# A state-space and gated-MLP block whose first part takes its order and its engines from a table in place of a planner

## The chip, the cores and the metric

One core of a Trainium2 chip. The time is that of one execution on the device in microseconds (us); the lower the better.

## The reference

The input x is 2048 rows of 640 numbers, all in float32. Six rows of modulation (shift, scale and gate, twice) come from one condition vector through a 640 x 3840 matrix. The block is then

```python
h = layernorm(x) * (1 + ca) + sa
x = x + ga * A(h)        # A: a long convolution along the rows, per channel
h = layernorm(x) * (1 + cb) + sb
x = x + gb * B(h)        # B: (silu(h @ w1) * (h @ w3)) @ w2, 640 -> 1728 -> 640
```

A builds, for each of the 640 channels, a kernel of 2048 taps, `K = 2 Re sum_n C[n] exp(A[n] dt l)` over 128 complex terms, convolves the channel with it by Fourier transforms of length 4096, and adds `h * D_skip`.

## The kernel before

The kernel has two parts. The **first part** computes the parameters, layernorm statistics and modulation, and then A for five blocks of 128 channels (b = 0 to 4). The **second part** adds the inverse transform to x, normalises again and does B; its instructions stand in an order of their own.

A block of the first part runs through these steps; the names in brackets are the tiles in the profile.

- *Generation*, eight chunks of 16 channels (`gen_tasks`, `gen_chunk`): GpSimd adds the phases (ph) and multiplies the decay factors out of two small tables (e, into yy and xx); ScalarE takes sines and one absolute value (tr, ph); VectorE does five multiplies (yy, xx); TensorE multiplies 32 pairs into kps; ScalarE copies kps to ks, and VectorE adds the skip term. The chunk's products need all five multiplies. Every tile of the ring (ph, xx, yy, tr, kps) has 2 or 3 buffers.
- *Tables* for the chunks: three sums and three smaller steps per half block (step, p), on GpSimd but for a few that either GpSimd or VectorE does; `al8`, a scaling by the row index (tiles al8, xs_al8, ks0) that ScalarE's exp needs, and `mag`, a product in place, each on GpSimd or VectorE.
- *Normalised input*, four pieces (`h_tasks`): load xq, normalise to hn (four instructions, on ScalarE or VectorE), multiply and add a row on VectorE (hn, hb), store to hs, and fetch all of it turned around into xb.
- *First transform* of h and of K, eight pieces each (`first_tasks`): TensorE to ps, copied to sp by ScalarE or VectorE.
- *Spectra*, eight groups (`spectra_tasks`): TensorE makes fh and fk, ScalarE copies fh to hz, VectorE multiplies them into fp (x0, x1, c), TensorE makes fz out of two groups, and two copies to zt by ScalarE or VectorE, each stored to zd in DRAM.

At the end of the first part, once the last chunk's product is done, `change` frees the generator's memory and issues the loads of the residual rows and of the inverse table (in all five loads, the residual's in four). For the first two weight tiles, 0 and 13, there are tasks for the loads (`fw`, raw tiles wr and w2r), the rounding on ScalarE (`fa`, to wh and w2h) and the subtraction on GpSimd (`fs`, to wl and w2l). `iz` reads zd back for the first rows, four loads each, and `ir` does their inverse on TensorE and adds them on VectorE. Weights 1 and 2 belong to the second part, but their loads stand among the first part's last stores on SyncE.

All first-part work is given as 1532 *tasks* (`Plan.add`): a name, one engine or several to choose from, how long it is taken to last on each, what must come before, a rank, and the buffers it takes and gives. `Plan.place` works out an order: it keeps a clock per engine, one for the port that GpSimd and VectorE share, and one for the DMA line, and of the tasks that could start soonest on each engine it takes the one with the least rank; where a task has two engines it takes the one that would be done first. The durations are constants in the calls of `add`, the ranks a list of 1532 numbers (`RANKS`). `Plan.run` then calls the tasks in that order. Because each engine's instructions are chained as they are called (`InOrder`, whose line 157 all of them bear in the profile), the order of the calls is the order on each engine: an instruction that waits holds up all that stand behind it on its engine.

Of the kernel before, what the change touches and what calls it, by code (L numbers as in the profile page):

```python
# [32 lines left out]
RANKS = """  # L33
# [67 lines left out]
FP = 2  # L101
# [64 lines left out]
class Engines:  # L166
    def __init__(self, k, nc):
        self.vector, self.scalar, self.gpsimd, self.tensor, self.sync = (
            InOrder(k, e) for e in (nc.vector, nc.scalar, nc.gpsimd, nc.tensor, nc.sync))


class Plan:

    LAG = dict(PE=0.2, DVE=0.18, ACT=0.2, POOL=0.15, SP=0.0)
    CHAIN = dict(DVE=0.12, ACT=0.12, POOL=0.07)
    NEAR, RATE, LAND, FLY, ISSUE, AWAY, TABLE = 0.1, 235e3, 1.3, 0.7, 0.06, 8, 1.28

    def __init__(self, **rings):  # L180
        self.tasks, self.n = {}, rings
# [1692 lines left out]
```

## Time and profile before

| | us |
|---|---|
| median of 3 runs | 973.91 (970.91 to 974.12) |
| the profiled execution | 976.3 |
| its span, first to last instruction | 974.5 |
| TensorE busy | 869.6 |
| VectorE busy | 717.6 |
| ScalarE busy | 517.2 |
| GpSimd busy | 334.6 |

In the profile PE is TensorE, PEld its weight loads, DVE VectorE, ACT ScalarE, POOL GpSimd, and SP SyncE, which issues the DMAs; SPq marks SyncE's own queue. A row of a timeline has the start in us, the length in us, the engine, the line, the operation, what it writes and reads, the shapes, and in brackets how long the engine had been idle and what ended that. A row of a group has the number of instructions, their busy time, the mean in ns of one, and the idle time before them. A row of a stretch of time has its limits and length, then the busy time of PE, PEld, DVE, ACT and POOL with the number of instructions, TensorE's granted clock, the DMA engines' busy share and GB/s. The first part takes the first 380 us or so; the generator's last product ends at 345.1 us.

### The profile page before, as it was taken

The page shows a single profiled execution, that of the slowest core. Times are in us where ns is not written, and L with a number is a line of the kernel's source. Part 1 is how long each engine was busy: PE and PEld are TensorE (multiplying, and loading weights), DVE is VectorE, ACT ScalarE, POOL GpSimd, SP SyncE. Part 2 cuts the span into 40 slices and gives each one's busy share as a digit, 9 for nine tenths or more (in the row PEclk, how much of TensorE's full clock was granted, in tenths as well). Part 3 has the DMA queues.
Part 4 walks back from the last instruction along what each step waited for, and adds up shares of the span by engine and source line. Part 5 has one row for each costly group of instructions (what it writes and reads, how often), then busy time and mean ns, then how long its engine had stood idle before and what let it go on. Part 6 is the DMA issues. An engine that isn't in the chain of part 4 may idle for free.

```text
span 974.5 us, 20145 instructions
## 1 busy us (share of the span) xinstructions
PE 869.6 (89%) x8017; PEld 691.6 (71%) x8017; DVE 717.6 (74%) x1300; ACT 517.2 (53%) x866; POOL 334.6 (34%) x345
## 2 busy tenths in 40 slices
PE   1454787879899998999999999999999999999997
PEld 1132665767788883667778888888888888888875
DVE  7998999999999954747775375567477777765763
ACT  6868788979888841522243243445234444445331
POOL 1797798879899512100000000000212222200000
PEclk9886898999999999999999999999999999999999
DMA  9955453722223278987522354223131112122242
GB/s 217 279 167 197 105 136 88 175 65 80 57 67 88 68 207 236 218 214 181 144 82 81 95 148 121 83 81 90 46 82 54 54 54 55 41 81 87 88 151 82
DMA packets 122822, 113.19 MB, mean 116 GB/s; under 512 B 11752, under 2 KB 106472, under 8 KB 121320
## 3 DMA queue, kind: packets, MB, share of 16 engines
q1 hardware_dynamic: 121992, 110.99, 42.2%
q8 instruction: 63, 1.03, 0.4%
q10 hardware_dynamic: 736, 0.92, 0.3%
q14 instruction: 31, 0.25, 0.1%
HBM read 90.91 MB, written 20.97 MB: 115 GB/s over the span
## 4 chain that ended last, share of the span: by engine, by line
PE 68%; DMA 12%; DVE 12%; ACT 4%; issue 3%; SPq 1%; POOL 0%; ACTq 0%; DVEq 0%; POOLq 0%
PE p L875 16%; PE acc L1122 16%; PE gu L1085 6%; PE gu L1087 6%; PE gu L1086 6%; PE ps L157 5%; PE kps L157 3%; DVE yy L157 3%; PE fk L157 3%; PE fz L157 3%; PE fh L157 2%; DMA sp<-in_w_mod 2%; DMA zd<-zt 2%; DMA xs<-in_x 2%; DVE xx L157 2%
## 5 line engine op out<-in xcount | busy, mean ns | idle before, releaser
L1085 PE MATMUL gu<-xh,wh 128*128 128x512 f32 x270 | 105.2, 393 | 0.9 <-ACT xh L667 0.7
L1087 PE MATMUL gu<-xh,wl 128*128 128x512 f32 x270 | 105.3, 390 | 0.0
L1086 PE MATMUL gu<-xl,wh 128*128 128x512 f32 x270 | 105.2, 390 | 0.0
L875 PE MATMUL p<-x,wch 128*128 128x512 f32 x312 | 92.6, 390 | 0.0
L157 POOL TENSOR_TENSOR yy<-e,e 128x512 f32<-128x512 f32 x80 | 86.2, 1095 | 17.5 <-PE kps L157 12.6
L894 POOL TENSOR_TENSOR ws<-wp 128x256 f32<-128x256 f32 x13 | 9.6, 740 | 228.7 <-DVE wcl L668 116.1
L157 POOL TENSOR_TENSOR ph<-p,p 128x1024 int32<-128x1024 int32 x40 | 79.0, 1974 | 5.7 <-ACT tr L157 5.0
L157 PE MATMUL kps<-yy,xx 128*32 128x64 f32 x2560 | 52.1, 238 | 27.3 <-DVE xx L157 24.0
L157 DVE TENSOR_TENSOR yy<-yy,tr 128x512 f32<-128x512 f32 (+1 forms) x80 | 75.3, 943 | 0.9 <-ACT tr L157 0.6
L157 PEld LDWEIGHTS kps<-yy,xx 128*32 128x32 f32 x2560 | 45.6, 118 | 37.0 <-issue 20.6
L779 ACT ACTIVATE wh<-wr 128x640 fp32r<-128x640 f32 x51 | 34.9, 731 | 64.3 <-PE gu L1086 51.6
L875 PEld LDWEIGHTS p<-x,wch 128*128 128x128 f32 x312 | 58.2, 188 | 12.6 <-ACT s L910 0.4
L1085 PEld LDWEIGHTS gu<-xh,wh 128*128 128x128 f32 x270 | 50.6, 188 | 11.7 <-ACT xh L667 1.0
L1087 PEld LDWEIGHTS gu<-xh,wl 128*128 128x128 f32 x270 | 50.7, 188 | 11.1 <-DVE wl L788 0.4
L1086 PEld LDWEIGHTS gu<-xl,wh 128*128 128x128 f32 x270 | 50.7, 188 | 10.5 <-DVE xl L668 0.2
L791 POOL MEMSET w2l<- 64x640 f32 x1 | 0.6, 633 | 165.5 <-PE acc L1122 165.5
L875 PE MATMUL p<-x,wcl 128*128 128x512 f32 x156 | 57.0, 389 | 0.0
L157 ACT ACTIVATE tr<-ph,hpi 128x512 f32<-128x512 f32 x80 | 54.7, 691 | 4.2 <-DVE xx L157 2.5
L157 DVE TENSOR_TENSOR xx<-tr,xx 128x512 f32<-128x512 f32 x80 | 54.3, 680 | 0.8 <-ACT tr L157 0.8
L912 DVE TENSOR_TENSOR s<-p,s 128x512 f32<-128x512 f32 x52 | 34.7, 682 | 26.9 <-ACT s L910 22.9
L157 ACT ACTIVATE tr<-ph 128x512 f32<-128x512 int32 x80 | 47.4, 599 | 12.7 <-DVE yy L157 5.8
L157 PE MATMUL ps<-wk,ks 128*64 128x128 f32 x640 | 41.9, 283 | 13.6 <-DVE ks L157 9.7
(367 smaller groups left out, 2303.1 us busy)
## 6 DMA issues: line engine op xcount, KB each, us to landing
wr<-in_w SPq DMA_DIRECT2D x52, 320.0 KB, 3.7
zd<-zt SPq DMA_DIRECT2D x39, 256.0 KB, 2.8
w2r<-in_w SPq DMA_DIRECT2D x26, 320.0 KB, 3.1
wp<-in_w SPq DMA_DIRECT2D x26, 320.0 KB, 3.2
wq<-in_w SPq DMA_DIRECT2D x26, 320.0 KB, 3.2
low<-zd SPq DMA_DIRECT2D x24, 320.0 KB, 6.6
xs<-in_x SPq DMA_DIRECT2D x16, 320.0 KB, 11.1
hs<-hb SPq DMA_DIRECT2D x20, 256.0 KB, 2.5
```

The costliest lines, as they stand in the source:

```text
L157: self.prev = self.k.order(f(*a, **kw), self.prev)
L779: self.nc.scalar.activation(wh[:, i], raw[:, i], AF.Copy)
L791: self.nc.gpsimd.memset(w2l[64:].bitcast(F32), 0.0)
L875: nc.tensor.matmul(to, t[:, o], y[:, k], start=start and k == i == 0, stop=stop and (k, i) == (n - 1, 2), skip_group_check=True)
L894: G.tensor_tensor(s[0], a21, a22, op=ALU.add)
L912: add = lambda o, bk, s: V.tensor_tensor(o, bk, s, op=ALU.add)
L1085: nc.tensor.matmul(pg, wh[:, k, :], xh[:, k, :], start=(k == 0), stop=False)
L1086: nc.tensor.matmul(pg, wh[:, k, :], xl[:, k, :], start=False, stop=False)
L1087: nc.tensor.matmul(pg, wl[:, k, :], xh[:, k, :], start=False, stop=(k == KT - 1))
L1122: nc.tensor.matmul(acc[k], *two(a, w), start=(m == 0 and i == 0), stop=(m == 12 and i == 2))
```

## The change

The tasks, their buffers and what each waits for stay as they are. The planner, with its durations and ranks, is gone. In place of `RANKS` stands `ORDER`, a list of the 1532 task numbers in the order in which they are called; a letter behind a number tells the engine where a task has a choice (a, d, p: ScalarE, VectorE, GpSimd). Of the table only the first line is shown; its numbers tell a reader nothing.

```diff
-RANKS = """
--1152 -1540 -1534 -1515 -1509 -1417 -1345 -1436 -1412 -1402 -1385 -1330 -1273 -1351 -1452 -1478 -1480 -1475 -1459 -1510 -1507
...
+ORDER = """
+1 2 7 13 79 78 80 4 86 81 41 14 19 82 20 42 84 21 15 83 22 16 150p 85 43 23 151 120 12 44 24 17 10 25 18 3 45 61 28 26 59 30
...
-    def __init__(self, **rings):
-        self.tasks, self.n = {}, rings
+    def __init__(self):
+        self.tasks = {}
...
-    def place(self, rank):
...
     def run(self):
 
-        T = self.tasks
-        found = [int(x) for x in RANKS.split()]
-        assert not found or len(found) == len(T)
-        self.order = self.place(dict(zip(T, found)) if found else {n: t[4] for n, t in T.items()})
-        for s, f, e, n in self.order:
-            if T[n][2]:
-                T[n][2](e)
+        T = list(self.tasks.items())
+        done = set()
+        for x in ORDER.split():
+            n, (engs, f, after) = T[int(x.rstrip("adp"))]
+            assert done.issuperset(after), (n, set(after) - done)
+            done.add(n)
+            if f:
+                f(dict(a="ACT", d="DVE", p="POOL")[x[-1]] if len(engs) > 1 else engs[0])
+        assert len(done) == len(T)
...
-        self.plan = plan = Plan(ph=2, xx=2, yy=2, tr=3, kg=2, f2=3, bank=4, hz=3, xq=2, fp=FP, zt=3, xs=4, st=1)
+        self.plan = plan = Plan()
```

What the table does to the queues: 54 tasks change engine. VectorE gets 13 more of the copies from ps to sp (it had 19 and gives back five for 18), six of the zt copies while four go to ScalarE, and loses nine normalisations for two. The scalings al80 and al81 go to GpSimd and al82 and al84 come to VectorE, with mag4; of the table copies three go to GpSimd and two come. On VectorE, the last piece of h for block 4 stands 64 us of its work earlier, by the traced durations. Nothing moves in the second part's own order. Three places follow in full.

The first is ScalarE at the end of the first part, in the kernel before. hz40 to hz47 are the copies of block 4's eight groups, zt401 the copy of its first fz; wh0_0 and wh0_13 are the roundings of weight tiles 0 and 13.

```order
L157 ACTIVATE hz40_4914<-fh40_4889 128x512
L157 ACTIVATE hz41_4937<-fh41_4916 128x512
L157 ACTIVATE hz42_4961<-fh42_4941 128x512
L157 ACTIVATE hz43_4974<-fh43_4951 128x512
L157 ACTIVATE zt400_5000<-fz400_4976 128x512
L157 ACTIVATE hz44_5024<-fh44_5004 128x512
L157 ACTIVATE hz45_5047<-fh45_5028 128x512
L157 ACTIVATE wh0_0_5049<-wr0_0_4864 128x640 x2
L157 ACTIVATE w2h0_0_5050<-w2r0_0_4867 128x640
L157 ACTIVATE hz46_5094<-fh46_5069 128x512
L157 ACTIVATE wh0_13_5102<-wr0_13_4899 128x640
L157 ACTIVATE w2h0_13_5103<-w2r0_13_4902 128x640
```

And the same place in the kernel after:

```order
L146 ACTIVATE hz40_4914<-fh40_4895 128x512
L146 ACTIVATE hz41_4925<-fh41_4905 128x512
L146 ACTIVATE wh0_13_4936<-wr0_13_4854 128x640
L146 ACTIVATE w2h0_13_4937<-w2r0_13_4857 128x640
L146 ACTIVATE hz42_4969<-fh42_4943 128x512
L146 ACTIVATE hz43_4981<-fh43_4958 128x512
L146 ACTIVATE wh0_0_4985<-wr0_0_4879 128x640 x2
L146 ACTIVATE w2h0_0_4986<-w2r0_0_4882 128x640
L146 ACTIVATE zt401_5026<-fz401_5003 128x512
L146 ACTIVATE zt400_5030<-fz400_5002 128x512
L146 ACTIVATE hz44_5033<-fh44_5017 128x512
L146 ACTIVATE zt410_5065<-fz410_5045 128x512
```

Weight 13 is now rounded behind the second hz copy and weight 0 behind the fourth; before, weight 0 stood behind the sixth and weight 13 behind the seventh.

The second place is SyncE from the loads that `change` issues on, in the kernel before. low<-in_x and low<-in_t_wd are the residual rows and the inverse table, wr and w2r the raw weights (of tiles 0, 13, 1 and 2), low<-zd the loads of iz, four each, and zd<-zt the stores of block 4.

```order
L157 DMA low_4848<-in_x 32x2560 x4
L157 DMA low_4848<-in_t_wd 128x2048
L157 DMA wr0_0_4864<-in_w1 128x5x128
L157 DMA wr0_0_4864<-in_w3 128x5x128
L157 DMA w2r0_0_4867<-in_w2 128x640
L157 DMA wr0_13_4899<-in_w1 128x5x64
L157 DMA wr0_13_4899<-in_w3 128x5x64
L157 DMA w2r0_13_4902<-in_w2 64x640 x2
L157 DMA low_4848<-zd_71 64x2x512 x4
L157 DMA zd_71<-zt400_5000 128x4x128
L157 DMA zd_71<-zt401_5002 128x4x128
L157 DMA zd_71<-zt410_5066 128x4x128
```

Behind these stand iz's other four loads, weight 1's three and then zt411's store. In the kernel after, from weight 0's w2 on:

```order
L146 DMA w2r0_0_4882<-in_w2 128x640
L665 DMA wr0_1_5429<-in_w1 128x5x128
L665 DMA wr0_1_5429<-in_w3 128x5x128
L670 DMA w2r0_1_5432<-in_w2 128x640
L146 DMA zd_71<-zt401_5026 128x4x128
L146 DMA zd_71<-zt400_5030 128x4x128
L665 DMA wr0_2_5519<-in_w1 128x5x128
L665 DMA wr0_2_5519<-in_w3 128x5x128
L670 DMA w2r0_2_5522<-in_w2 128x640
L146 DMA zd_71<-zt410_5065 128x4x128
L146 DMA low_4848<-zd_71 64x2x512 x8
L146 DMA zd_71<-zt411_5094 128x4x128
```

Weight 13's loads now stand ahead of weight 0's, both still directly behind the five loads of `change`; weight 1's loads stand ahead of block 4's first store and weight 2's ahead of the third; and all eight loads of iz stand in one piece between the third store and the fourth (zt411, the task z4.1.o1). On TensorE and VectorE the two units of `ir` move from the middle of block 4's last groups to behind its last fz.

The third place is VectorE in the first block, chunks 5 and 6 (tiles with 80 and 96 in their names; tr4 marks a chunk's last multiply). Before:

```order
L157 SCALAR_TENSOR_TENSOR yy_96_809<-yy_96_809,tr0_96_823 128x16x32
L157 TENSOR_TENSOR hn_814<-hn_814,rw_87 128x512
L157 TENSOR_TENSOR yy_96_809<-yy_96_809,tr0_96_823 128x16x32
L157 TENSOR_TENSOR xx_96_808<-tr1_96_826,xx_96_808 128x512
L157 TENSOR_TENSOR hb01_844<-hn_728,rw_87 128x512
L157 TENSOR_TENSOR yy_96_809<-yy_96_809,tr3_96_842 128x1024
L157 TENSOR_TENSOR xs_al8_851<-al_126,j8_103 128x1024
L157 TENSOR_TENSOR hb02_858<-hn_814,rw_87 128x512
L157 TENSOR_TENSOR xx_80_734<-tr4_80_833,xx_80_734 128x512
```

And after:

```order
L146 TENSOR_TENSOR hn_658<-hn_658,rw_87 128x512
L146 TENSOR_TENSOR yy_80_708<-yy_80_708,tr3_80_810 128x1024
L146 TENSOR_TENSOR hb01_820<-hn_658,rw_87 128x512
L146 TENSOR_TENSOR xx_80_707<-tr4_80_813,xx_80_707 128x512
L146 TENSOR_TENSOR xx_96_804<-tr1_96_822,xx_96_804 128x512
L146 SCALAR_TENSOR_TENSOR yy_96_805<-yy_96_805,tr0_96_817 128x16x32
L146 TENSOR_TENSOR ks0_128<-kps_410,dsk_74 128x4 x2
```

Chunk 5's last multiply stood behind four multiplies of chunk 6 and the scaling of block 1 (xs_al8); now it stands ahead of all of chunk 6, and that scaling is on GpSimd.

More of the change, by code (lines that the diff above doesn't have):

```diff
@@ new lines @@
+851 589 329a 461 467 464 590 339a 469 591 354 449 584 465 326 475 454 355a 470 466 455 327a 471 492 479 334 593d 456 480 472
+335a 481 476 457 585 866 356 594 473 477 482 373 484 357 586 595 478 358 474 485 596 852a 493 486 375 359 494 487 483 856 496
+495 488 374 501 497 509 489 597 867a 360 503 361 510 490 502 861 362 498 491 376 511 853 363 512 499 377 513 854 701 500 504
+855 364 519 514 505 515 702 378 506 520 526 862a 365 518 366 527 516 868 530 367 529 517 535 507 528 508 522 521 543 536 523
@@ new lines @@
+406 411 575 735 404 736 576 725 721 733 1138 737 559 412 1139 415 734 722 741 1141a 608 416 727 614 609a 417 1414 615a 743 738
+418 1399 742 616 1142 739 1143 723 744 740 1144 602 749 617a 728 1415a 612 745 766 603d 729 613d 753 1130 626 1416 1400a 752
+1417 746 627d 1418 975 770 624 1401 1125 754 1402 419 755 760 1403 1131d 625a 978p 769 618 422a 423 976 420d 619a 1409 1132
+979 1126a 606 977 1133 607d 421 598 1134 750 1127 628 599a 751 1128 758 1129 604 1410a 767 629d 759 600 980 775 605a 768 981
@@ new lines @@
+662a 661 828 687 823 663 673 681 674 688 824 675 814 985p 682 983 829 825 683 835 815 830 838 676 684 989 839 843 840 816 685
+689 841 677d 837 679a 686 678 831 836 680 690 896 845 832 986 1247 691 987 892 897d 984 692 890 893d 990 693 988 891d 833 844
+992 846 876 991 993 694d 894 1248d 695 886 696d 877a 999 994 697 884 895d 842 1000 995 1006 874 847 887a 998 848 1145 875a
+885d 996 898 849 1007 1001 997 904 1010 1009 1002 1011 900 850 1015 905 1008 899d 1012 902 1023 901d 1003 1013 1016 903a 1017
@@ new lines @@
+1244a 1362 1242a 1223 1245 1373 1243 1377 1438 1363 1385 1386 1378 1436 1445a 1383 1439d 1387 1379 1437a 1393 1384 1388 1391
+1224 1392 1380 1389 1381 1364 1390 1394 1446 1227a 1395 1440 1228 1447a 1225d 1396 1441d 1226 1448 1397 1398 1520 1525 1450
+1449d 1426 1522 1451a 1442 1521 1427d 1452 1443d 1458 1453 1454 1459 1460 1526 1455 1456 1469 1461 1527 1475 1457 1470 1462
+1471 1476 1463 1523 1472 1477 1473 1464 1474 1524 1478 1479 1486 1467a 1480 1465a 1468 1487 1466 1488 1481 1489 1490 1491 1492
@@ L99 @@
+1482a 1483 1503 1493 1528 1494 1504 1484a 1495 1530 1505 1496 1509 1497 1506 1511 1510 1485 1507 1512 1508 1513 1498 1514 1515
+1501a 1499d 1500 1502 1529 1518a 1519 1516a 1531 1517
 """
@@ L172 @@
 class Plan:
-    LAG = dict(PE=0.2, DVE=0.18, ACT=0.2, POOL=0.15, SP=0.0)
-    CHAIN = dict(DVE=0.12, ACT=0.12, POOL=0.07)
-    NEAR, RATE, LAND, FLY, ISSUE, AWAY, TABLE = 0.1, 235e3, 1.3, 0.7, 0.06, 8, 1.28
-    def __init__(self, **rings):
-        self.tasks, self.n = {}, rings
+    def __init__(self):
+        self.tasks = {}
     def add(self, name, eng, took, f, after=(), rank=0.0, port=False, take=(), give=(), table=None, dma=None):
         assert name not in self.tasks, name
-        take = [(r, name + "".join(x), k) for r, k, *x in take]
@@ L272, in run @@
-    def run(self):
-        T = self.tasks
-        found = [int(x) for x in RANKS.split()]
-        assert not found or len(found) == len(T)
-        self.order = self.place(dict(zip(T, found)) if found else {n: t[4] for n, t in T.items()})
-        for s, f, e, n in self.order:
-            if T[n][2]:
-                T[n][2](e)
+            eng, f = (eng,), f and (lambda e, f=f: f())
+        self.tasks[name] = (eng, f, tuple(after))
+    def run(self):
+        T = list(self.tasks.items())
[7 more added lines that the diff above has]
+        assert len(done) == len(T)
```

115 lines of the change are left out of this document (35 added, 80 removed), and 64 rows, old and new, of the table RANKS.

## The prediction

> **What bounds the kernel now.** I read the page first, then the busy times by stretch, then the chain of waits from 340 us on, and last the single instructions of VectorE, ScalarE and the DMA queue around the places where the new order differs.
>
> ```profile
> span 974.5 us, 20145 instructions
> PE 869.6 (89%) x8017; PEld 691.6 (71%) x8017; DVE 717.6 (74%) x1300; ACT 517.2 (53%) x866; POOL 334.6 (34%) x345
> ```
>
> The execution took 976.3 us, 1.8 more than its span and 2.4 (0.25%) more than the median, 973.91. I add differences to the median. The three runs before lie 3.2 us apart, so about 0.5% (4.9 us) is the least that a measurement tells from no change.
>
> The averages hide two halves. These are the busy times of the first part, in four stretches:
>
> ```profile
> 0.00:20.00 20.00, 1.30 (x5) 0.93 (x5) 13.83 (x35) 11.89 (x23) 1.68 (x19) 1.00 0.92 199
> 20.00:120.00 100.00, 55.66 (x920) 36.30 (x922) 92.18 (x175) 77.15 (x146) 81.60 (x77) 0.81 0.66 194
> 120.00:280.00 160.00, 134.60 (x2754) 113.00 (x2754) 152.87 (x286) 136.44 (x230) 141.11 (x142) 0.96 0.39 99
> 280.00:340.00 60.00, 59.42 (x1218) 49.10 (x1208) 58.57 (x106) 50.59 (x89) 49.91 (x46) 1.00 0.29 73
> ```
>
> The third figure after the stretch's length is VectorE (the order is PE, weight load, VectorE, ScalarE, GpSimd). From 20 to 340 us VectorE is idle for 7.8 + 7.1 + 1.4 = 16.4 us in all. It is the bound, and TensorE joins it from 280 us on (59.4 of 60). So a new order can win at most 16.4 us of waits there, plus what VectorE no longer has to do before the last generated chunk is ready. After that a second regime begins, in the chain of waits:
>
> ```profile
> 344.03 1.10 PE kps L157 x61
> 362.88 0.70 DVE zt L157
> 364.09 5.65 DMA zd<-zt
> 369.81 7.25 DMA zd<-zt
> 377.13 0.60 ACT zt L157
> 378.07 6.04 DMA zd<-zt
> 384.85 3.48 DMA low<-zd
> 388.46 1.51 PE iy L653 x10
> ```
>
> The last product of the generator ends at 345.1 (kps, 344.03 + 1.10). Block 4 then runs through its spectra (fh, fk, fz), and the chain passes to the stores of zd: a copy out of fz waits until an older store has released its zt buffer. The last store lands at 384.1, 39.0 us after that product, and only then can the feed-forward part read zd. What follows is issued in the same order in both kernels, so I take it as unchanged. The forecast is the sum of two shifts: that of the last product, and that of the 39.0 us.
>
> **The work VectorE does ahead of the last product.** Durations by kind, 0 to 400 us:
>
> ```profile
> L157 DVE COPY sp<-ps 128x512 f32<-128x512 f32 x19 | 12.7, 682 | 2.6 <-PE ps L157 2.5
> L157 DVE TENSOR_SCALAR hn<-xq,rs_y_h,rs_n_h 128x128 f32<-128x128 f32 x44 | 18.1, 412 | 1.6 <-ACT sp L157 0.3
> L157 DVE TENSOR_TENSOR xs_al<-al,j 128x1024 f32<-128x1024 f32 x1 | 2.8, 2817 | 0.0
> L157 DVE TENSOR_TENSOR ks<-al,j 128x1024 f32<-128x1024 f32 x1 | 1.2, 1218 | 0.0
> L157 DVE TENSOR_TENSOR e<-e,mag 128x512 f32<-128x512 f32 x2 | 2.2, 1077 | 0.0
> L157 DVE TENSOR_SCALAR p<-pB 128x128 int32<-128x128 int32 x4 | 1.1, 273 | 0.0
> ```
>
> The new table gives VectorE 13 more copies out of ps and 4 more out of fz ahead of block 4's spectra, and leaves 5 of these 17 behind its last generator multiply: 12 x 0.68 = +8.2 us. It takes away 7 normalisations of four instructions: 7 x 4 x 0.412 = -11.5. Two scalings by the row index (al8) leave, 1.22 and 2.82, and two come back for later blocks; I price these at the mean, 2.02 each, so they cancel (between 1.22 and 2.82 each, that is -1.6 to +1.6). One magnitude product comes, +1.1, and one of the copies of p goes, -0.3. Sum -2.5; ScalarE takes the other side and has room (136 of 160 us). Instructions overlap by some 0.06 us, so **-2.4**.
>
> The 2.82 us stand beside running GpSimd work, the 1.22 us where GpSimd was idle. The Trainium skill, SBUF — State Buffer, section on the two separate sides, says that VectorE and GpSimd share one port pair under an exclusive lock, which an instruction of VectorE with two SBUF inputs also needs; these rows agree. By that rule both scalings would come back at 2.82 and the term would be -0.8.
>
> **The start.** The rows of GpSimd and ScalarE where the first chunk begins:
>
> ```profile
> 34.14 2.28 POOL L157 TENSOR_TENSOR ph<-p,p 128x1024 int32<-128x1024 int32 x1
> 36.45 0.60 ACT L157 ACTIVATE tr<-ph 128x512 f32<-128x512 int32 x1 [0.56 <-POOL ph L157]
> ```
>
> and two groups of the first 400 us:
>
> ```profile
> L157 POOL TENSOR_TENSOR step<-p 128x128 int32<-128x128 int32 x18 | 7.8, 432 | 1.4
> L157 ACT ACTIVATE xs<-xs,h_nm 128x640 f32<-128x640 f32 x12 | 9.8, 814 | 0.3 <-DVE h_nm L157 0.3
> ```
>
> Six of the small table instructions for the block's second half now stand ahead of this phase on GpSimd (6 x 0.43 = 2.6 us), and four more squares and two sines of the next chunk ahead of the first chunk's last sine on ScalarE (4 x 0.81 + 2 x 0.60 = 4.5 us). VectorE has parameter steps to put beside part of that, and they now all come ahead of the first chunk's multiplies. I take 1.5 us lost, between 0 and 4: **+1.5**. SyncE's loads of the start are dealt out anew as well, but the same bytes, and 0.26 MB of tables more, stand ahead of the last block of x, so the statistics end about when they did.
>
> **A stall that goes.** VectorE between 88 and 98 us:
>
> ```profile
> 88.04 2.82 DVE L157 TENSOR_TENSOR xs_al<-al,j 128x1024 f32<-128x1024 f32 x1
> 91.38 0.67 DVE L157 TENSOR_TENSOR xx<-tr,xx 128x512 f32<-128x512 f32 x1
> 94.23 0.17 DVE L157 TENSOR_TENSOR ks<-kps,dsk 128x4 f32<-128x4 f32 x1 [1.39 <-PE kps L157]
> 97.77 0.69 DVE L157 COPY sp<-ps 128x512 f32<-128x512 f32 x1 [2.18 <-PE ps L157]
> ```
>
> Chunk 5's last multiply (the xx of 91.38) stood behind four instructions of chunk 6 and the long al8, so TensorE got both products late and VectorE then waited 1.39 + 2.18 = 3.6 us for them. In the new order that multiply comes before chunk 6, and the al8 is GpSimd's. I take the whole of it, between -3.6 and 0: **-3.6**.
>
> The other 16.4 - 3.6 = 12.8 us of waits are scattered in pieces under 1.5 us; the orders of five queues cross differently at each (block 4's normalised input, for one, is made 64 us of VectorE's work earlier), and I find no rows that say whether more go than come. I take 0, between -8 and +8.
>
> **The hand-over.** ScalarE after the last product:
>
> ```profile
> 353.43 0.60 ACT L157 ACTIVATE hz<-fh 128x512 f32<-128x512 f32 x1 [1.25 <-PE fh L157]
> ...
> 357.17 0.60 ACT L157 ACTIVATE zt<-fz 128x512 f32<-128x512 f32 x1 [2.17 <-PE fz L157]
> 361.52 1.35 ACT L157 ACTIVATE wh<-wr 128x640 fp32r<-128x640 f32 x2
> 364.92 0.60 ACT L157 ACTIVATE hz<-fh 128x512 f32<-128x512 f32 x1 [1.42 <-issue]
> ```
>
> The first two weight loads as the tile's view from 348 us has them, then the page's line of all such loads, and the busy row whose last figures are the DMA's share and its GB/s:
>
> ```profile
> L157 SPq DMA_DIRECT2D wr<-in_w x2: 385/454/524, 348.6 to 349.0; - x2
> DMA to landing us min/median/max: 10.5/10.7/11.0
> wr<-in_w SPq DMA_DIRECT2D x52, 320.0 KB, 3.7
> 360.00:380.00 20.00, 18.84 (x144) 10.40 (x140) 15.48 (x40) 7.30 (x12) 8.28 (x6) 1.00 1.07 304
> ```
>
> The rounding of the first weights on ScalarE (wh) stood late, behind six hz copies. Now weight 13's stands between block 4's second and third hz copy, and weight 0's ahead of the first copies out of fz. But the weights are issued behind the residual rows and the inverse table (2.4 MB): the first two landed 10.5 and 11.0 us after issue, at 359.1 and 360.0, where most such loads take 3.7 us (page, part 6). The new order has the same 2.4 MB ahead. So, in the old times, weight 13's rounding would end at about 362 (w2 lands about 1 us after w1 and w3, an estimate from 320 KB at 304 GB/s), and the third hz copy, at 353.43 before, comes at 362: 8.5 us late, with TensorE's fz and all later copies behind it. Weight 0's then ends at about 365.5, and the first fz copies at about 366.5 where they ended at 357.8: 8.7 us late. On SyncE the load of weight 1 now stands ahead of these copies' stores and waits until GpSimd has subtracted weight 13, at about 364; that is earlier than the copies, so it costs nothing by itself.
>
> Against it stands what no longer interrupts the rest of the block:
>
> ```profile
> 366.35 1.04 PE L157 MATMUL iy<-low 128*64 128x512 f32 x2 [0.62 <-DMA low<-zd]
> 368.67 0.69 DVE L157 TENSOR_TENSOR low<-iy,low 128x512 f32<-128x512 f32 x1 [0.56 <-PE iy L157]
> 370.13 1.63 DVE L157 BATCH_NORM_STATS2 st_n<-low 128x6 f32<-128x128 f32 x8
> ```
>
> The inverse's first unit held TensorE from 366.35 and VectorE from 368.67 to 371.8 (370.13 + 1.63); it now comes after the block's last fz. That and the roundings give back some 4 us. Last copy 8.7 - 4 = 4.7 late. Its store landed 6.4 us after the copy ended (377.13 + 0.60 to 384.1), behind a full DMA queue (1.07 busy, 304 GB/s); with the queue drained I take 4.7: net **+3.0**. Low end -3, if the weights land early enough; high end +9: eight loads of zd (2.1 MB, 6.9 us at 304 GB/s) now stand ahead of the store z4.1.o1, for whose buffer the last copy waits, where four stood.
>
> The Trainium skill, DMA: Bandwidth & Descriptors, section on queues, rings and completion order, says that on each DMA engine descriptors are consumed in ring order; the 10.7 us against 3.7 agree. It speaks against moving the rounding forward: weights cannot pass what was issued ahead of them.
>
> **Sum:** -2.4 + 1.5 - 3.6 + 0 + 3.0 = -1.5 us, that is 974.8 for the profiled execution and 972.4 for the median.
>
> **Rivals.**
>
> *The waits go too (faster).* The new table was made from measured durations; if engines meet each other better all along, 7 of the 12.8 us go: -1.5 - 7 = -8.5, 965.4 us. For it: the old planner's own costs are short (0.6 us for a multiply that takes 0.68), so its queues cross by chance. Against it: VectorE is already 95.5% busy from 120 to 280 us and 97.6% after, and TensorE shares the bound from 280 us on, so VectorE's gain late there shows only if TensorE got its work earlier too. The same time comes out if the weights land as most do, 3.7 us after issue: then no rounding waits and the hand-over gains 4.
>
> *The hand-over costs far more (slower).* If weight 13's loads, in pieces of 64 columns, land 2 us later than I took, each step behind them moves 2 us on, weight 2's load waits for GpSimd's subtraction and stops SyncE's queue, and the eight loads push z4.1.o1 back: +10 in place of +3, total +5.5, 979.4 us. It decides once the last zd store lands more than 48 us after the last product (39.0 + 9.4).
>
> *The change does nothing.* The order changes on every queue and 54 tasks change engine, so this is out.
>
> **How the numbers follow.** No change (972.4, own range 969 to 977): 0.43. Faster by over 4.9 us: 0.34; these are the rival's waits, with the stall's full gain. Slower by over 4.9 us: 0.23, of which 0.15 is the hand-over and the rest new waits of VectorE between 110 and 340 us (up to +8). The range, 962 to 981, leaves out about one in ten on each side: below, more than three quarters of the scattered waits would have to go; above, both the hand-over's high end and a worse start.
>
> **What the new profile would show.** Last kps product at 340 to 343 us instead of 345.1. No wait of VectorE over 1 us between 90 and 98 us. ScalarE idle for 6 us or more ahead of the first wh, by a DMA, and the third hz copy behind it. The last zd store landing 40 to 44 us after the last kps product. TensorE after 400 us as before, shifted. I am wrong if VectorE's idle time between 20 and 340 us leaves 9 to 19 us, if wh waits for nothing, or if the feed-forward part changes its length.

## The result: 14.7 us slower, and the profile after

| | before | after |
|---|---|---|
| median of the runs made side by side, us | 974.01 (4 runs) | 988.68 (4 runs) |
| ratio, 95% interval | | 1.016 (1.0138 to 1.0182) |
| the profiled execution's span, us | 974.5 | 986.8 |
| last product of the generator ends, us | 345.1 | 351.7 |
| first iy of the feed-forward part starts, us | 387.3 | 401.2 |

The forecast was 972.4, with 962 to 981 as its range. The kernel is slower than that range allows. The profiles are 12.3 us apart and the medians 14.7, because the profiled execution of the kernel before (976.3) was 2.4 us longer than its median. The first page of the kernel after:

```profile
span 986.8 us, 20117 instructions
PE 876.1 (89%) x8017; PEld 698.1 (71%) x8017; DVE 712.9 (72%) x1287; ACT 520.9 (53%) x879; POOL 336.1 (34%) x345
```

VectorE has 4.7 us less to do in all (712.9 for 717.6), as the table meant, and the kernel still takes longer. The busy times, in the stretches that the prediction read:

```profile
0.00:20.00 20.00, 5.62 (x23) 3.12 (x23) 14.29 (x34) 12.26 (x22) 4.13 (x20) 1.00 0.90 239
20.00:120.00 100.00, 52.32 (x834) 35.62 (x834) 83.08 (x167) 79.62 (x151) 86.42 (x83) 0.80 0.67 187
120.00:280.00 160.00, 132.35 (x2676) 110.43 (x2680) 149.46 (x267) 131.70 (x232) 128.82 (x129) 0.91 0.37 95
280.00:340.00 60.00, 59.37 (x1242) 49.98 (x1235) 57.64 (x105) 50.08 (x89) 52.47 (x47) 1.00 0.26 64
```

VectorE's idle time from 20 to 340 us is now 16.9 + 10.5 + 2.4 = 29.8 us, where it was 16.4. From 20 us up to the generator's last product it is 30.5 us, where it was 20.1, while VectorE has 3.8 us less to do there: 10.4 - 3.8 = 6.6, by which that product ends later. The product's row in the kernel after:

```profile
350.52 1.17 PE L146 MATMUL kps<-yy,xx 128*32 128x64 f32 x64
```

Two shorter stretches show where it came from. Before:

```profile
20.00:60.00 40.00, 22.07 (x274) 10.87 (x275) 38.20 (x73) 34.80 (x74) 31.00 (x29) 0.87 0.92 266
140.00:180.00 40.00, 32.24 (x554) 26.61 (x556) 37.73 (x75) 32.79 (x56) 33.95 (x37) 0.87 0.50 132
```

And after:

```profile
20.00:60.00 40.00, 14.89 (x187) 8.48 (x187) 33.00 (x67) 29.76 (x66) 32.03 (x31) 0.83 0.99 253
140.00:180.00 40.00, 25.21 (x430) 18.31 (x434) 32.53 (x59) 29.58 (x50) 31.74 (x32) 0.76 0.27 74
```

VectorE (third figure behind the length) was busy for 5.2 us less in each. The second stretch has one clear cause. First SyncE's queue there:

```profile
154.74 4.52 SPq L146 DMA_DIRECT2D xq<-in_x  x8
159.35 0.38 SPq L146 DMA_DIRECT2D hs<-hb  x1
```

The piece that this store takes away, on VectorE:

```profile
156.31 0.68 DVE L146 TENSOR_TENSOR hb<-hn,rw 128x512 f32<-128x512 f32 x1
```

Then ScalarE, VectorE and TensorE, one row each from their timelines:

```profile
162.15 0.60 ACT L146 ACTIVATE hz<-fh 128x512 f32<-128x512 f32 x1 [3.68 <-DMA hs<-hb]
162.78 0.69 DVE L146 TENSOR_TENSOR fp<-fk,hz 128x512 f32<-128x512 f32 x1 [3.33 <-ACT hz L146]
166.93 3.78 PE L146 MATMUL fz<-fp,wz 64*128 64x512 f32 x8 [8.45 <-DVE fp L146]
```

The tiles hb (a finished piece of the normalised input, stored to hs) and hz (the copy of a spectrum) are allocated from one ring of three buffers (`ring`, tag "hz", line 1050 of the kernel after). The piece hb was finished at 157.0 us. Its store stood behind eight loads of xq on SyncE, was issued at 159.35 and had landed by 162.1; only then could ScalarE write the next hz. VectorE waited for that hz with the last sum of the spectrum before it (a combination into fp) standing behind, and TensorE's fz waited for that sum.

The hand-over also came out longer. ScalarE behind the last product:

```profile
357.46 0.60 ACT L146 ACTIVATE hz<-fh 128x512 f32<-128x512 f32 x1 [0.31 <-PE fh L146]
366.33 0.74 ACT L146 ACTIVATE wh<-wr 128x640 fp32r<-128x640 f32 x1 [8.28 <-DMA wr<-in_w]
367.48 0.74 ACT L146 ACTIVATE w2h<-w2r 128x640 fp32r<-128x640 f32 x1 [0.41 <-DMA w2r<-in_w]
368.12 1.06 ACT L146 ACTIVATE hz<-fh 128x512 f32<-128x512 f32 x2
```

And TensorE's end of the first part, after:

```profile
385.08 3.67 PE L146 MATMUL fz<-fp,wz 64*128 64x512 f32 x14 [0.96 <-DVE fp L146]
388.68 3.86 PE L146 MATMUL iy<-low 128*64 128x512 f32 x16
394.15 7.13 PE L146 MATMUL awake<-low,ident 128*128 128x512 f32 x16 [1.61 <-DVE low L146]
401.22 1.14 PE L555 MATMUL iy<-low 128*64 128x128 f32 x12
```

and before:

```profile
377.64 7.13 PE L157 MATMUL awake<-low,ident 128*128 128x512 f32 x16
387.33 0.87 PE L653 MATMUL iy<-low 128*64 128x128 f32 x6 [2.55 <-DMA low<-zd]
```

The sixteen products called awake compute nothing; they are there to keep TensorE busy while it waits for data, for the sake of its clock. Before, they ended 2.55 us ahead of the data from zd. Now both units of the inverse stand behind the last fz, awake ends at 401.28, and the first iy waits for nothing but its own engine. The first iy comes 49.5 us after the last product (351.7 to 401.2); before, 42.2 (345.1 to 387.3).

So the profile's 12.3 us are 6.6 ahead of the last product, 7.3 from there to the first iy, and -1.6 behind it (974.5 - 387.3 = 587.2; 986.8 - 401.2 = 585.6).

### The profile page after: what moved, and what is told of

Its sections match the earlier page's. It is cut to its first block, busy times and chain, and to the rows that moved or that the text cites. A ratio compares the mean times of both kernels' runs of the same rounds, so it can differ in the third digit from the quotient of the medians.

```text
span 986.8 us, 20117 instructions
## 1 busy us (share of the span) xinstructions
PE 876.1 (89%) x8017; PEld 698.1 (71%) x8017; DVE 712.9 (72%) x1287; ACT 520.9 (53%) x879; POOL 336.1 (34%) x345
## 4 chain that ended last, share of the span: by engine, by line
PE 72%; DVE 13%; ACT 4%; DMA 4%; issue 3%; POOL 2%; SPq 1%; DVEq 0%; ACTq 0%; POOLq 0%
PE acc L1024 16%; PE p L777 16%; PE gu L987 6%; PE gu L989 6%; PE gu L988 6%; PE ps L146 4%; PE fz L146 4%; PE kps L146 3%; DVE yy L146 3%; PE fh L146 2%; PE fk L146 2%; DVE fp L146 2%; DVE xx L146 2%; PE iy L555 2%; SPq L146 1%
## 5 line engine op out<-in xcount | busy, mean ns | idle before, releaser
L146 PE MATMUL fz<-fp,wz 64*128 64x512 f32 x160 | 46.6, 672 | 15.1 <-DVE fp L146 9.6
L988 PEld LDWEIGHTS gu<-xl,wh 128*128 128x128 f32 x270 | 50.7, 188 | 10.4 <-DVE xl L570 0.2
```

The lines of the kernel that those rows point to most:

```text
L146: self.prev = self.k.order(f(*a, **kw), self.prev)
L988: nc.tensor.matmul(pg, wh[:, k, :], xl[:, k, :], start=False, stop=False)
```

## The experiments

Seventeen kernels ran. Each is written in the form of the kernel after, with another table; only one changes anything else. Tables were cut at a task: the order of one kernel up to it, then what is left in the order of the other. Given as a table, the old planner's order issues what the kernel before issues, instruction for instruction. A ratio is to the kernel before on the same chip, with its 95% interval; the kernel after stands at 1.016. A profile's points move too: the run "tail_only" issues the same instructions as before up to the last product, and its last product reads

```profile
341.16 1.39 PE L146 MATMUL kps<-yy,xx 128*32 128x64 f32 x64
```

so it ends at 342.55, 2.6 us sooner than before's 345.1. Points that differ by less than that say nothing.

### Four cuts: which part loses

tail_only and tail_back: cut at the generator's last product (task g4.7.p).

```diff
 tail_only:  before up to g4.7.p | after behind it
 tail_back:  after up to g4.7.p  | before behind it
```

> The order of before up to the generator's last product (task g4.7.p), then what is left in the order and on the engines of after. Theory: the new order loses in three places that add up: VectorE's waits until the last product (+6.6 us), the hand-over from that product to the last zd store (42.7 us instead of 39.0: +3.7), and the stretch from that store to the first iy product of the feed-forward part (6.9 us instead of 4.4: +2.5). This kernel has the last two: last product at 345, last store 42 to 43 us behind it, time 974 + 6.2 = 980 us (978 to 982). Rival, the whole loss before the last product and the late stretch only inherits it: 974 us.

> The order and engines of after up to the generator's last product (task g4.7.p), then what is left in the order of before. Theory (losses in three places that add up): last product at 351 to 352, last zd store 39 us behind it, time 974 + 6.6 = 981 us (979 to 983). Rival, the hand-over is where the loss comes from and the first part's 6.6 us would be taken up by slack behind it: 974 to 976 us. Rival, the late stretch only inherits: 988 us.

tail_only took 980.15 us, 1.0083 (1.0055 to 1.0110); tail_back 981.08, 1.0077 (1.0046 to 1.0107). The two excesses make 1.0160 together, which is the kernel after's own ratio. About half of the loss lies ahead of the last product and half behind it, and neither hides in the other.

start_only and start_back: cut at the first block's last product (task g0.7.p, about 100 us).

```diff
 start_only:  after up to g0.7.p  | before behind it
 start_back:  before up to g0.7.p | after behind it
```

> The order and engines of after up to the last product of the generator's first block (task g0.7.p, at about 100 us), then what is left in the order of before. Theory: the start loses 5.4 us (VectorE behind its old place by that much, corrected for its work, at the first block's last multiply) and nothing gives them back, since VectorE bounds what follows: 974 + 5 = 979 us (977 to 981). Rival, the start's loss is taken up by later waits and the loss is made between 105 and 176 us: 974 us.

> The order of before up to the last product of the generator's first block (task g0.7.p), then what is left in the order and on the engines of after. Theory: the start's 5.4 us are won back, the rest of the loss stays: 988.7 - 5.4 = 983 us (981 to 985). Rival, the start's loss would have been taken up anyway: 988 us.

start_back took 983.94, 1.0103 (1.0070 to 1.0137): as expected, about 5 us are won back. start_only took 988.16, 1.0148 (1.0116 to 1.0180), 10 us more than expected. Its trace shows why it tells nothing of the start alone:

```profile
100.00:140.00 40.00, 25.98 (x424) 23.26 (x424) 25.15 (x47) 27.12 (x46) 23.56 (x21) 0.70 0.28 68
```

Just behind the cut VectorE is idle for 14.9 of 40 us. I take it that what after's start had left undone was not what before's rest expects to be done; no run shows it by itself. A cut can add a seam of its own, so I read this one no further.

### Order without engines, engines without order

```diff
 engines_only:  before's order, after's engine for the 54 tasks
 order_only:    after's order, before's engine for the 54 tasks
```

> The order of before, word for word, with only the 54 tasks that change engine on their new engine. VectorE has 3.3 us less to do until the last product (315.5 busy instead of 318.8 in the two traces). Theory, the loss comes from the new order and not from the engines: last product 1 to 3.3 us earlier than 345.1 and 971 to 973 us. Rival, the new engines are what makes the queues meet badly: VectorE's idle time from 20 us to the last product goes from 20.1 to 28 us or more, and the time is 978 us or more.

> The order of after, word for word, with the 54 tasks that change engine back on their old engine. If the loss sat in the order alone, this is as slow as after or slower by the 3.3 us of VectorE's work: 988 to 993 us. If it sat in the engines, 974 to 978 us. What I expect after the run with the engines alone (993.5 us): order and engines were dealt out together, and either alone is worse than both: 993 us or more.

engines_only took 993.50, 1.0205 (1.0190 to 1.0221); order_only 997.05, 1.0232 (1.0207 to 1.0256). The theory for engines_only fell by 20 us: either half alone is worse than both. VectorE's waits from 20 to 345 us in engines_only:

```profile
DVE sp L146 <- PE ps L146: 8.4, 5, 2.6
DVE hn L146 <- ACT hn L146: 4.7, 4, 1.6
DVE ks L146 <- ACT ks L146: 4.6, 2, 3.0
```

(total, times, longest). VectorE got thirteen sp copies more, in the places where ScalarE used to take them, and its waits for the products of all its sp copies come to 8.4 us, in pieces up to 2.6, where they were 2.5 in all. An engine dealt out anew needs its place in the queue with it.

### The stall at 158 us

fix_stall is after with two moves; h2.1.a is the add that makes the piece hb, h2.1.o its store, h4.1.l and h3.3.l two loads of xq (four DMAs each), w0.3 and w0.4 two of block 0's spectra.

```diff
 SyncE
-z0.0.o1  h4.1.l  h3.3.l  h2.1.o
+z0.0.o1  h2.1.o  h4.1.l  h3.3.l
 VectorE
-w0.3.x1 ... w0.4.x0  w0.4.x1  w0.4.c  w0.3.c
+w0.3.x1  w0.3.c ... w0.4.x0  w0.4.x1  w0.4.c
```

> After, with one store (hs<-hb of block 2's last added chunk) moved on SyncE ahead of eight loads of xq, and the last combination of block 0's third spectrum moved on VectorE from behind the next spectrum's to right behind its own products. Theory: ScalarE waited 3.7 us at 158 to 162 us for the buffer that this store held, VectorE 3.3 us behind it and TensorE 8.45 us behind that; VectorE's idle time from 140 to 180 us goes from 7.5 us to 3 to 4, the last product comes 3 to 4 us earlier than 351.7 and the time is 984.5 to 986. Rival, the buffer is taken up by the next task in the ring and the wait only moves: idle 6 to 8 us and 988 to 989 us.

982.78 us, 1.0094 (1.0079 to 1.0109): about 6 us won by two moves among 1532 tasks, a little more than expected. The same places in its trace:

```profile
140.00:180.00 40.00, 28.13 (x518) 21.05 (x513) 36.86 (x67) 33.72 (x60) 33.99 (x35) 0.79 0.34 93
```

```profile
155.91 0.36 SPq L146 DMA_DIRECT2D hs<-hb  x1
156.44 4.01 SPq L146 DMA_DIRECT2D xq<-in_x  x8
```

```profile
158.42 0.60 ACT L146 ACTIVATE hz<-fh 128x512 f32<-128x512 f32 x1 [1.07 <-DMA hs<-hb]
```

```profile
158.09 2.97 PE L146 MATMUL fz<-fp,wz 64*128 64x512 f32 x8 [0.56 <-DVE fp L146]
```

The store goes out 3.4 us sooner, ScalarE's wait falls from 3.68 to 1.07 us, TensorE's from 8.45 to 0.56 (two more, of 1.82 and 2.50, come behind it), and VectorE's idle time in the stretch from 7.5 to 3.1. The last product ends at 347.1 instead of 351.7. So the loss at this place is shown; how much of it the late store made, and how much the sum that stood behind the next spectrum on VectorE, no run separates.

### The hand-over

fix_fa is after with the roundings of the first two weights further back on ScalarE (w4.2.h to w4.6.h are block 4's third to seventh hz copy, fa1 and fa0 the roundings of weights 13 and 0; GpSimd's subtractions go with them):

```diff
 ScalarE
-w4.1.h  fa1  w4.2.h  w4.3.h  fa0  z4.0.v1  z4.0.v0  w4.4.h  z4.1.v0  w4.5.h  w4.6.h
+w4.1.h  w4.2.h  w4.3.h  z4.0.v1  z4.0.v0  w4.4.h  z4.1.v0  w4.5.h  fa1  w4.6.h  fa0
```

> After, with the rounding of the first two weights on ScalarE moved from behind block 4's second and fourth hz copy to behind the sixth and seventh (and GpSimd's subtractions behind them). Theory: ScalarE no longer stands 8.3 us for a load with the third hz copy behind it; block 4's spectra come up to 8 us sooner, and since the weights and the last unit of the inverse still have to come, half of it shows: last zd store visible 37 to 40 us after the last product instead of 42.7, time 983 to 986. Rival, the hand-over is set by the two inverse units behind the last fz and by the loads, not by the rounding: 988 to 989 us.

982.40 us, 1.0081 (1.0057 to 1.0105): 6 to 8 us won, a little more than expected. ScalarE and TensorE there:

```profile
360.47 0.60 ACT L146 ACTIVATE hz<-fh 128x512 f32<-128x512 f32 x1 [2.12 <-PE fh L146]
```

```profile
386.51 7.13 PE L146 MATMUL awake<-low,ident 128*128 128x512 f32 x16 [1.22 <-DVE low L146]
395.40 0.87 PE L555 MATMUL iy<-low 128*64 128x128 f32 x6 [1.76 <-DMA low<-zd]
```

The third hz copy starts at 360.5 instead of 368.1, awake ends at 393.6, and the first iy waits for its data again. It comes 43.4 us after the last product of this run (ended at 352.0), where it was 49.5 in the kernel after and 42.2 before.

no_awake is after without the line that issues the sixteen products:

```diff
-        self.awake(nc.tensor, po.tile([P, 512], F32, name="awake0", tag="acc4"), 8)
```

> After, without the sixteen products (eight calls) that only keep TensorE's clock up ahead of the feed-forward part. Theory: they stand between 394.2 and 401.3 us on TensorE, and the data of the first iy has landed at 398.5, so that it starts 2 to 3 us sooner and the time is 986 to 987. Rival, the clock granted behind it falls and takes it back or more: 988 to 992 us.

985.97 us, 1.0113 (1.0087 to 1.0139; it leaves out work that computes nothing):

```profile
388.91 3.90 PE L146 MATMUL iy<-low 128*64 128x512 f32 x16
397.82 3.30 PE L555 MATMUL iy<-low 128*64 128x128 f32 x16 [5.00 <-DMA low<-zd]
```

In the kernel after, the data could have been used at about 398 and was at 401.2. The sixteen products cost about what they overhang, some 3 us. What they are there for shows as well: without them TensorE's granted clock is 0.72 from 396 to 400 us (1.00 in the kernel after), and the sixteen iy products take 3.30 us where they take 1.73 behind awake in the next run.

fix_ir puts the inverse's first unit back between the block's last spectra:

```diff
 SyncE
-z4.0.o1  z4.0.o0  z4.1.o0  iz0  iz1  z4.1.o1
+iz0  z4.0.o1  z4.0.o0  z4.1.o0  iz1  z4.1.o1
 TensorE
-w4.6.k  w4.7.f  w4.7.k  z4.2.z  z4.3.z  ir0  ir1
+w4.6.k  ir0  w4.7.f  w4.7.k  z4.2.z  z4.3.z  ir1
```

> After, with the inverse's first unit (its product iy, and the four loads of zd for it) put back to where before has it, between the block's last but one and last spectrum. Theory: with both units behind the last fz, TensorE reaches the sixteen products that keep its clock up (7.1 us) only at 394.2, and the first iy of the feed-forward part, whose data has landed by 398.5, waits until 401.2; with one unit earlier these products end 1.5 to 2 us sooner, and the time is 986 to 987.5. Rival, the loads of zd set that point: no change, or 1 us more because the unit holds VectorE ahead of the last products, 988 to 990 us.

990.13 us, 1.0168 (1.0153 to 1.0183): nothing won, the theory failed. Its rows:

```profile
388.52 6.01 PE L146 MATMUL fz<-fp,wz 64*128 64x512 f32 x14 [0.67 <-DVE fp L146]
396.36 7.13 PE L146 MATMUL awake<-low,ident 128*128 128x512 f32 x16
403.42 1.73 PE L555 MATMUL iy<-low 128*64 128x128 f32 x16
```

With the unit among the spectra the last fz ends at 394.5 instead of 388.75, and awake 2.2 us later than in the kernel after. So the late place of the inverse's units is not a mistake of the table by itself: in fix_fa both units stand behind the last fz too, and the first iy waits for its data. The place costs once ScalarE's wait has pushed the last fz back.

### The start

Where the first chunk begins, GpSimd and VectorE in the kernel after (p and step are table tiles, ph the chunk's phase; the yy row is the first multiply):

```profile
34.84 0.88 POOL L146 COPY p<-pS 128x128 int32<-128x128 int32 x1
35.80 0.72 POOL L146 TENSOR_TENSOR step<-p 128x128 int32<-128x128 int32 x1
...
38.91 0.88 POOL L146 COPY p<-pB 128x128 int32<-128x128 int32 x1
39.66 1.94 POOL L146 TENSOR_TENSOR ph<-p,p 128x1024 int32<-128x1024 int32 x1
```

```profile
43.68 0.69 DVE L146 SCALAR_TENSOR_TENSOR yy<-yy,tr 128x512 f32<-128x512 f32 x1 [4.17 <-POOL yy L146]
```

The six table steps took 4.8 us (34.84 to 39.66), not the 2.6 of the prediction; VectorE did two-input work beside them. Three runs, and two more below, looked for what to undo. t0.1.0, t0.1.3 and t0.1.1 are the table steps, s, m and ph the first chunk's sines, multiplies and phase, sq squares of the statistics, x0 to x3 loads of x, w0 to w4 loads of the modulation weights, wk and dsk two of the tables.

```diff
 fix_start, GpSimd
-t0.1.0  t0.1.3  g0.0.ph ... g0.1.z0  t0.1.1  g0.1.z1
+g0.0.ph ... g0.1.z0  g0.1.z1  t0.1.0  t0.1.3  t0.1.1
 start_mix: fix_start, and
+ScalarE: each of g0.0.s0 to s4 behind one of the squares and sums from sq10 on
+VectorE: each of g0.0.m0 to m4 behind one of the last parameter steps
 start_loads: start_mix, and on SyncE
-ld T w0 dsk x1 wk w3 x0 x2 w1 w2 x3 w4
+ld T x1 x0 w0 x2 w1 w2 w3 dsk x3 w4 wk
```

> After, with three steps of the block's second table (copy and sums on GpSimd, 34.84 to 39.66 us, and one of 0.85) moved from ahead of the first chunk's phase to behind the second chunk's magnitudes. Theory: these 4.8 us on GpSimd make the first product late (51.8 instead of 45.9); the phase then starts at 34.8, but ScalarE's squares hold the first sine until 40.4 where it now starts at 41.6, so that the first product comes 2 to 4 us earlier and the time is 984.5 to 987. Rival, ScalarE's squares alone set the start, or later waits take it up: first product within 1 us of 51.8, 988 to 989 us.

> After, with GpSimd's table steps behind the second chunk's magnitudes, the first chunk's five sines on ScalarE dealt out among the squares instead of behind them, and the first chunk's five multiplies on VectorE among the last parameter steps instead of behind them, as in before. Theory: each of the three engines held the first chunk by itself, so only all three together bring it forward; first product at 46 to 48 us instead of 51.8, and 983 to 986 us. Rival, the pair of VectorE and GpSimd is full until 52 us whichever order stands there (two-input work of the one lengthens the other's): the first product comes earlier but VectorE has as much left behind it, 988 to 989 us.

> The run before it (start_mix) with SyncE's loads of x ahead of those of the modulation weights and the other tables, as in before. Theory: ScalarE waited 4.7 us for them at 22 to 27 us and its statistics are what the first sines stand among; 1 to 3 us less than the run before it. Rival, the statistics have slack and the modulation comes later: no change, or up to 2 us more.

fix_start: 988.87, 1.0161 (1.0143 to 1.0179), nothing won. start_mix: 987.06, 1.0134 (1.0108 to 1.0160), not to be told from the kernel after's 1.016 (1.0138 to 1.0182). start_loads: 998.01, 1.0247 (1.0225 to 1.0270), 11 us lost. fix_start's stretch:

```profile
20.00:60.00 40.00, 15.58 (x188) 8.38 (x189) 37.73 (x68) 29.81 (x68) 32.76 (x32) 0.91 0.95 231
```

VectorE's idle time fell from 7.0 to 2.3 us, and as many of its instructions (68 for 67) took 37.73 us where they took 33.00: the wait was given back as longer instructions. The last parameter step ahead of the first multiply, in the kernel after and in fix_start:

```profile
38.72 0.79 DVE L146 SCALAR_TENSOR_TENSOR xb<-xb,dt 128x512 f32<-128x512 f32 x1
```

```profile
41.93 2.32 DVE L146 SCALAR_TENSOR_TENSOR xb<-xb,dt 128x512 f32<-128x512 f32 x1
```

The same instruction takes 2.9 times as long beside a phase of GpSimd (41.31 to 43.70 in fix_start) as beside its small steps. The first multiply starts at 44.18, no sooner than in the kernel after (43.68). start_loads failed for another reason: TensorE

```profile
26.18 1.93 PE L146 MATMUL pm<-sp,sc 128*32 128x512 f32 x8 [17.46 <-DMA sp<-in_w_mod]
28.04 1.12 PE L146 MATMUL ptp<-ident,e 128*128 128x128 f32 x4
```

waited 17.5 us at a modulation product for its weights, which now come later, and the transposes that the tables need stood behind it. The order of the loads goes with the order of TensorE.

### Do the causes add up

```diff
 two:    fix_stall and fix_fa together
 three:  two, and start_mix
 four:   three, and the second chunk's s0 to s2 and m0, m2 ahead of block 2's last squares and mean
 best:   before up to g0.7.p | fix_stall's order up to g4.7.p | before behind it
```

> After with both of the edits that won by themselves: the store and the combination of the stall, and the roundings behind the sixth and seventh hz copy. If they are independent, 988.7 - 5.9 - 6.3 = 976.5 us (975 to 978). If the hand-over takes up what the stall gives: 981 to 983 us.

> The run before it (two) with the start of start_mix. If the start's 5 us come back and add up: 971 to 974 us, with before or just ahead of it. If the start's edit is worth nothing: 976.5 us, as the run before it.

> The run called three with the second chunk's first three sines on ScalarE ahead of the last four squares, and its first two multiplies on VectorE ahead of block 2's mean. If a chain of holders on ScalarE is what is left of the start's loss, VectorE's idle time from 20 to 60 us goes from 4.8 to 2.5 us or less and the time is 974 to 977 us. If VectorE and GpSimd are simply full there, 978.5 us as the run before it.

> Before up to the first block's last product, then after's order and engines with the store and the combination moved as in the run on the stall, up to the generator's last product, then what is left as in before. Theory: the three losses add up, and each undoing was worth by itself 4.7 (start), 5.9 (stall) and 7.6 us (hand-over) against after's 988.7: 970 to 974 us, no slower than before, possibly faster by what VectorE no longer does (3 us). Rival, orders and engines of different tables don't fit together, as in the run with after's start and before's rest (988 us): 978 us or more.

two: 978.29, 1.0054 (1.0033 to 1.0076). three: 978.74, 1.0051 (1.0033 to 1.0069). four: 980.43, 1.0079 (1.0056 to 1.0103). best: 975.41, 1.0003 (0.9990 to 1.0016).

The two mended causes take 10.6 of the kernel after's 16 thousandths away; independent, they would have taken 6.6 + 7.9 = 14.5. The difference, 3.9, is within what the four intervals leave open (about 4), so whether they add up in full is not shown. Mending the first and second chunk by hand adds nothing to it, so neither what was moved on GpSimd, VectorE and ScalarE in three nor the squares in four is the start's cause by itself. With the start and the end of before around it, after's middle with the stall mended takes as long as before: no further loss shows outside these three places. Nor does a gain: the theory's 970 to 974 us were not reached, and up to the last product VectorE waits 3.6 us less there than before (16.5 for 20.1) but is busy for 4.7 more (309.7 for 305.0). No table that I tried is faster than before.

## Why the prediction was wrong, point by point

- **VectorE's work ahead of the last product, -2.4.** Right in size: from 0 us to that product VectorE was busy for 315.5 us where it was 318.8 (union of its rows in the two traces), -3.3. But it was not worth that in time: the places that lost, lost by waits. One of its prices came out lower. The two scalings that came back took 1.40 and 1.22 us, not 2.82, though GpSimd worked beside them: the second began 0.12 us ahead of GpSimd's phase (173.28 and 173.40), while the one of 2.82 in the kernel before had begun 0.21 us behind a phase (88.04 and 87.83). "By that rule both scalings would come back at 2.82" left out which of the two instructions starts first; these rows fit a price that goes by it.
- **The start, +1.5 (0 to 4).** Too small: 5.2 us more idle time in 20 to 60 us, the first multiply starting 5.3 us late (38.4 before), and 5 us in start_back. Six GpSimd steps were counted at the group's mean of 0.43 and took 0.8 each; but moving them back won nothing (fix_start), so their length is not shown to be the loss. That no single move wins it back was not foreseen; what makes it stays open.
- **The stall at 92 to 98 us, -3.6.** The two waits went, as said, and others came in their place: 1.41 us at 91.6 for ScalarE's ks, 1.22 at 99.5, and 2.95 at 103.8 for the modulation's columns. From 60 to 100 us VectorE is idle for 6.2 us where it was 4.5. The gain did not arrive, and the sign "no wait of VectorE over 1 us between 90 and 98 us" failed at 91.6.

```profile
91.61 0.17 DVE L146 TENSOR_TENSOR ks<-kps,dsk 128x4 f32<-128x4 f32 x1 [1.41 <-ACT ks L146]
99.51 0.69 DVE L146 TENSOR_TENSOR xx<-tr,xx 128x512 f32<-128x512 f32 x1 [1.22 <-ACT tr L146]
103.81 0.30 DVE L146 TENSOR_SCALAR cols<-pv 128x5 f32<-128x5 f32 x3 [2.95 <-PE pv L146]
```

- **The other 12.8 us of waits, 0 (-8 to +8).** This step failed most: the idle time of VectorE from 20 to 340 us, which the prediction wanted between 9 and 19 us, is 29.8. "I find no rows that say whether more go than come": no row of before could, but the order of after could. The store of a piece behind eight loads on SyncE, and a ring that the piece shares with a spectrum, stand in the order itself, and a load's issue takes 0.5 us there (4.52 for eight). By fix_stall this one place is worth 6 us, with the sum on VectorE that was moved together with the store.
- **The hand-over, +3.0 (-3 to +9).** The mechanism was right on ScalarE and the stores: ScalarE stood 8.28 us ahead of the first wh, "8.5 us late" in the forecast, and the third hz copy behind it came at 368.1. Before, the feed-forward's loads of zd were issued 39.0 us after the last product; here it is 42.7 (394.4), for a forecast of 42.0. The step that failed is what it left out, TensorE: "what follows is issued in the same order in both kernels, so I take it as unchanged". Between the block's last fz and the first iy stand the two inverse units and 7.1 us of awake, and with the last fz at 388.75 they end behind the data. The hand-over lost 7.3 us in place of 3.0. fix_fa wins 6.1 of it back by taking ScalarE's wait away; the overhang of 3 us (no_awake) is a part of the same loss.
- **The rivals.** "The hand-over costs far more" named the right side and the wrong measure: its point, a last store more than 48 us after the last product, was not reached. "The waits go too" fell: waits came.
- **The range.** Its upper end took one bad case at a time. The start's 4, VectorE's +8 and the hand-over's +9 lay open at once, and the kernel lost at all three: 5.2 and 5.2 us of VectorE's time and 7.3 us of the hand-over.

The rule that was cited, the Trainium skill, DMA: Bandwidth & Descriptors, section on queues, rings and completion order, agrees with the trace: the first two wr loads landed 10.3 to 10.4 us after issue behind the 2.4 MB, ScalarE waited 8.28 us for them, and fix_fa won 6 to 8 us by not asking for them early.

## What to carry to other kernels

An order and its engines are one thing: half of a table that was dealt out together costs more than the whole (20 and 22 us here, for 14.7). Before pricing a new order by engine, follow each shared ring of buffers in it: what frees the buffer, on which queue, and what stands ahead of that there; here a store behind eight loads on SyncE kept ScalarE waiting, VectorE behind it, and TensorE behind both. And at a hand-over between parts, follow every engine up to the first instruction of the next part, the one that does nothing useful included.

## What the runs showed of the hardware

- Idle time can be given back as length. The same VectorE instruction took 2.32 us beside a phase of GpSimd and 0.79 beside its small steps, these small steps took 0.72 to 0.88 us beside VectorE's work and 0.41 to 0.45 in their new place, and 4.7 us of waits became 4.7 us of work (fix_start). The Trainium skill, SBUF — State Buffer, section on the two separate sides, tells of the port that the two engines share; these rows agree. That the port is what makes the start cost 5 us is not shown.
- TensorE's granted clock was low behind stretches in which TensorE did little. In the kernel after it had no work from 160 to 164 us; from 164 to 172 the clock was 0.50, and eight fz products took 3.78 us. Eight more in the same trace, at a clock of 1.00,

```profile
177.98 1.99 PE L146 MATMUL fz<-fp,wz 64*128 64x512 f32 x8
```

took half of that. In fix_stall, without the wait of 8.45 us, the clock was 1.00 up to 164 us and 0.50 from 164 to 168, around waits of 1.82 and 2.50 us; over 140 to 180 us it came to 0.79 for 0.76. If the wait is what lowers the clock, a stall is paid for twice; what the second payment is worth no run here shows.
